# Turning the first batch's blocks by 16-bit halves and a transposing DMA instead of on TensorE

## The chip, the cores and the metric

One core of one Trainium2 chip runs the whole program. The metric is device microseconds of one execution; the time quoted for a kernel is the median of its runs.

## What is computed

The reference chains three layers for 2 batches of 768 positions with 512 channels. Banded attention gives x. A mixer follows, and then a second mixer with a rotation. The part that matters here is the first mixer:

```python
xt = x.transpose(0, 2, 1)
h = np.maximum(xt @ w_tok1, 0.0) @ w_tok2
u = x + h.transpose(0, 2, 1)
h2 = np.maximum(u @ w_ch1, 0.0) @ w_ch2
return (u + h2)
```

The product with `w_tok1` is called the first mixing product below, that with `w_tok2` the second. The product with `w_ch1` is the up-projection, that with `w_ch2` the down-projection.

## The kernel before

**Tiling.** A batch is held as x[b], six row blocks of 128 positions by 512 channels. Every large product is made of three passes: both operands are split into a high part (rounded to fp32r) and a low part (what is left), and `mm3` (L96) issues high*high, high*low and low*high.

**The stages around the change.** Attention runs in 24 units (each two blocks of one pair of heads), written out by hand in `attention_band`. The PE work of later layers is hung into its last units by the table `fill`: `token_part` is one step of the first mixing product (program names mm1, shown as mm), `token_row` one row block of the second (mm2, also shown as mm), whose result VectorE adds into x (L768, x<-mm). So batch 0 is through its second mixing product when attention ends, and batch 1 gets its own in `token_mix2`, behind the end of the If block that chooses between two forms of attention.

**The turn.** The up-projection needs u with channels on the partitions. Batch 0 is turned by `turn_row`: four 128x128 transposes on TensorE (L799, ut<-ident,x) into one PSUM bank of the tag "t" (two banks, which attention's own transposes t use too), then `evac_split`: ScalarE writes the high part (L706, xh<-ut), VectorE the low part (L712, xl<-ut,xh). The results lie in `ut[0]`, in two pieces: positions 0 to 511 (blocks 0 to 3) and 512 to 767 (blocks 4 and 5). Batch 1 is turned later, under batch 0's channel mix, in another way: GpSimd copies the block apart into 16-bit halves (L779, `halves_out`), the SP queue issues a transposing DMA (L783), GpSimd joins the halves again (L789, `halves_join`), then ScalarE writes the high part (L792) and VectorE the low part (L793).

**Conversions.** Weights come as 64-bit words and pass through jobs: a load on the SP queue (L125), two scaling steps on ScalarE (L139, L140), two steps on VectorE (L145, L148), an addition on GpSimd (L149), the high part on ScalarE (L157), the low part on VectorE (L160). Each call of `tick()` moves every running job one phase on and starts one more. Jobs of the channel mix are started by `token_mix2` (three ticks) and then by `up`, behind each of its two evacuations.

**The channel mix.** `up(b, k)` makes 128 hidden columns in two PSUM tiles gp of the tag "t" (two banks, so a third tile waits until the first is evacuated); each is evacuated by ScalarE (L706, g<-gp) and VectorE (L708). `down` accumulates into six banks (h).

All engines run their instructions in the order in which the program is written; nothing is rescheduled.

## Time and profile before

| | us |
|---|---|
| median of 3 runs (492.0 to 493.21) | 492.08 |
| the profiled execution, its own time | 493.28 |
| span of that execution, first to last instruction | 491.5 |
| PE (matmul) busy | 484.3 of 491.5 |
| DVE / ACT / POOL busy | 317.4 / 262.9 / 180.8 |

In a timeline a row shows start and duration in us from the start of the span, engine, line, operation, the tiles as out<-in, shapes and a count; what stands in square brackets is the engine's idle time ahead of it and what ended that. Median and profiled execution are different runs: differences worked out on the span are carried over to the median.

### The profile page before, as it was taken

To read this page: it belongs to the slowest core of one execution; us is meant where nothing else is said; L and a number is where in the kernel's file an instruction comes from. 1 tells how busy PE (TensorE), PEld (TensorE's weight loads), DVE (VectorE), ACT (ScalarE), POOL (GpSimd) and SP (SyncE) were. 2 spreads that over 40 slices of the span, in tenths; PEclk is the share of its full clock that TensorE was granted. 3 is DMA by queue.
4 is the path that set the end of the run, shared out by engine and by line. 5 is a ranking of instruction groups with operands and counts; after the bars stand their busy time and mean duration, and the time that the engine had idled before them with its cause. 6 is when DMAs were issued, how large, how long until landed. Compare 5 with 4: busy or idle time off the path is not lost.

```text
span 491.5 us, 7645 instructions
## 1 busy us (share of the span) xinstructions
PE 484.3 (99%) x2836; PEld 412.3 (84%) x2836; DVE 317.4 (65%) x671; ACT 262.9 (53%) x482; POOL 180.8 (37%) x187
## 2 busy tenths in 40 slices
PE   8999999999999999999999999999999999999997
PEld 4788888787888888888888888888888889988896
DVE  4688787854776689506656564687998866351442
ACT  6888777723565554204569464646776566322010
POOL 7345534430443575401323241334554633333000
PEclk9999999999999999999999999999999999999999
DMA  6687863401454545302444222524210101000012
GB/s 194 202 261 219 280 209 119 129 2 50 134 172 107 158 137 143 94 1 85 147 133 149 87 56 60 141 87 104 68 23 22 44 22 23 21 23 22 23 71 101
DMA packets 49022, 50.66 MB, mean 103 GB/s; under 512 B 20944, under 2 KB 39888, under 8 KB 48976
## 3 DMA queue, kind: packets, MB, share of 16 engines
q1 hardware_dynamic: 48976, 50.08, 34.6%
q8 instruction: 25, 0.41, 0.3%
q14 instruction: 21, 0.17, 0.1%
HBM read 42.21 MB, written 3.15 MB: 92 GB/s over the span
## 4 chain that ended last, share of the span: by engine, by line
PE 83%; DVE 5%; ACT 5%; POOL 3%; DMA 2%; issue 1%; DVEq 0%; SPq 0%; POOLq 0%; ACTq 0%
PE gp L96 20%; PE h L96 18%; PE y L96 13%; PE v L96 7%; PE mm L96 7%; PE o L406 5%; PE th L96 5%; PE t L484 4%; PE s L437 4%; DMA k<-k 2%; POOL base L319 1%; ACT cut_xt L789 1%; DVE x L1061 1%; DVE w L1154 1%; POOL s L1180 1%
## 5 line engine op out<-in xcount | busy, mean ns | idle before, releaser
L149 POOL TENSOR_TENSOR cvt<-cvt,cvs 128x512 int32<-128x512 int32 (+1 forms) x57 | 75.1, 1318 | 177.2 <-DVE cvt L148 144.0
L96 PE MATMUL h<-wc,g 128*128 128x512 f32 x432 | 101.7, 389 | 0.0
L96 PE MATMUL gp<-xh,wc 128*128 128x512 f32 (+1 forms) x384 | 97.1, 335 | 0.0
L96 PEld LDWEIGHTS h<-wc,g 128*128 128x128 f32 x432 | 79.6, 188 | 15.2
L96 PEld LDWEIGHTS gp<-xh,wc 128*128 128x128 f32 x384 | 67.2, 189 | 8.6 <-DVE g L708 0.2
L708 DVE SCALAR_TENSOR_TENSOR g<-gp,g 128x512 fp32r<-128x512 f32 (+1 forms) x48 | 26.7, 556 | 63.4 <-ACT g L706 63.1
L96 PE MATMUL gp<-xl,wc 128*128 128x512 f32 (+1 forms) x192 | 64.3, 335 | 0.0
L96 PE MATMUL y<-wri,s 128*128 128x256 f32 (+1 forms) x288 | 52.0, 335 | 0.2 <-POOL s L1180 0.2
L96 PE MATMUL y<-wri,z 128*128 128x256 f32 (+1 forms) x288 | 51.9, 335 | 0.0
L706 ACT ACTIVATE g<-gp 128x512 fp32r<-128x512 f32 (+1 forms) x48 | 23.4, 486 | 53.2 <-PE gp L96 53.2
L96 PEld LDWEIGHTS y<-wri,s 128*128 128x128 f32 x288 | 44.7, 189 | 6.4 <-POOL s L1180 0.4
L96 PEld LDWEIGHTS y<-wri,z 128*128 128x128 f32 x288 | 44.6, 188 | 5.9
L484 PE MATMUL t<-ident,e 128*128 128x128 f32 x176 | 48.1, 285 | 0.4 <-ACT at L496 0.4
L145 DVE SCALAR_TENSOR_TENSOR cvs<-cvt,cvs 128x512 int32<-128x512 int32 (+1 forms) x57 | 44.8, 787 | 0.1
L96 PEld LDWEIGHTS gp<-xl,wc 128*128 128x128 f32 x192 | 36.0, 188 | 4.7
L450 DVE CUSTOM_DVE_ANT_0 e<-s,base 128x256 f32<-128x256 f32 (+1 forms) x96 | 32.9, 397 | 9.1 <-PE s L437 7.1
L484 PEld LDWEIGHTS t<-ident,e 128*128 128x128 f32 x176 | 31.7, 184 | 8.1 <-issue 2.3
L139 ACT ACTIVATE cvt<-raw 128x512 f32<-128x512 f32 (+1 forms) x57 | 37.2, 653 | 2.2 <-issue 2.2
L140 ACT ACTIVATE cvs<-raw 128x512 int32<-128x512 uint16 (+1 forms) x57 | 37.4, 656 | 0.0
L96 PE MATMUL th<-s,xt 128*128 128x512 f32 x144 | 34.9, 391 | 0.0
L1157 ACT ACTIVATE w<-w 128x512 f32<-128x512 f32 x12 | 7.6, 632 | 49.4 <-DVE w L1154 49.4
L406 PE MATMUL o<-v,at 128*128 128x65 f32 x192 | 32.3, 252 | 0.0
(111 smaller groups left out, 839.9 us busy)
## 6 DMA issues: line engine op xcount, KB each, us to landing
raw<-w_ch SPq DMA_DIRECT2D x28, 512.0 KB, 4.1
raw<-w_tok SPq DMA_DIRECT2D x21, 512.0 KB, 4.2
k<-k SPq DMA_DIRECT2D x7, 480.0 KB, 5.6
v<-v SPq DMA_DIRECT2D x8, 384.0 KB, 3.7
out<-o SPq DMA_DIRECT2D x11, 256.0 KB, 2.0
q<-q SPq DMA_DIRECT2D x7, 384.0 KB, 4.7
raw<-w_theta SPq DMA_DIRECT2D x4, 512.0 KB, 4.0
a<-v SPq DMA_DIRECT2D x8, 240.0 KB, 4.5
```

What stands on the lines that cost most here:

```text
L96: self.nc.tensor.matmul(out, lhsT=a, rhs=b, start=first and i == 0, stop=last and i == n - 1)
L139: nc.scalar.activation(out=f(t), in_=f(top), func=AF.Copy, scale=2.0**-111)
L140: nc.scalar.activation(out=s, in_=nxt, func=AF.Copy, scale=2.0**-13)
L145: nc.vector.scalar_tensor_tensor(out=s, in0=t, scalar=-(1 << 31), in1=s, op0=ALU.bitwise_and, op1=ALU.bitwise_or)
L149: nc.gpsimd.tensor_tensor(out=t, in0=t, in1=s, op=ALU.add)
L406: self.nc.tensor.matmul(po[:, j * OW : j * OW + D + 1], lhsT=at, rhs=v[:, j * (D + 1) : (j + 1) * (D + 1)], start=first, stop=last,)
L437: nc.tensor.matmul(ps[j][:, ii, c0:], lhsT=t["q"][pj, i * P : (i + 1) * P], rhs=kf[pj, i * KW - P + c0 : i * KW + P], start=True, stop=True,)
L450: nc.vector.tensor_tensor_reduce(out=e, in0=ps[j][:, ii, c0:], in1=self.base[2 * hp + j][min(i, 1)], op0=ALU.add, op1=ALU.min, scale=-SCAL ...
L484: nc.tensor.transpose(pt[:, ii, c, :], e[j][:, ii, c * P : (c + 1) * P], self.ident)
L706: nc.scalar.activation(out=hi, in_=ps, func=AF.Relu if relu else AF.Copy)
L708: nc.vector.scalar_tensor_tensor(out=lo, in0=ps, scalar=0.0, in1=f(hi), op0=ALU.max, op1=ALU.subtract)
L1157: nc.scalar.activation(out=a, in_=t, func=AF.Abs)
```

## The change

Batch 0's blocks are no longer turned on TensorE. `turn_row` and `turn_rows` are gone, with their 24 transposes and 6 evacuations. In `token_mix2`, behind the If, all six blocks are cut into halves by GpSimd (`columns_out`), each followed by its transposing DMA on the SP queue; behind batch 1's second mixing product all six are joined (the first four by GpSimd, the last two by ScalarE) and split into high and low parts; the three ticks stand behind all that. The scratch lies in places that later hold converted weights. The first mixing product of batch 1 finishes its first half before its second half begins, and the second mixing product's first three rows are made in two passes, so that the first pass needs only that first half.

```diff
-            for s in range(4):
-                fill[N - 2 + s].append(columns(s))
-            for tb in range(NT):
-                for s in range(NS - 2):
-                    fill[N + 1].append(mix1(1, tb, s, "s"))
+            for s in range(NS - 2):
+                fill[N + 1].append(mix1(1, 0, s, "s"))
...
             for tb in range(NT):
-                for s in range(NS - 2, NS):
+                for s in range(0 if tb else NS - 2, NS):
                     mix1(1, tb, s, "s")()
-            for s in range(4, NS):
-                columns(s)()
...
-    def token_row(self, tag, h1, b, s):
-
-        ps = self.ps.tile([P, E], F32, name="mm2_%d_%d" % (b, s), tag=tag)
+    def token_row(self, tag, h1, b, s, parts=range(NT)):
+
         cs = slice(s * P, (s + 1) * P)
+        if 0 in parts:
+            self.mm2[b, s] = self.ps.tile([P, E], F32, name="mm2_%d_%d" % (b, s), tag=tag)
+        ps = self.mm2[b, s]
...
-                for t in range(NT)
+                for t in parts
             ],
-        )
-        x = self.x[b][:, s, :]
-        self.nc.vector.tensor_tensor(out=x, in0=ps, in1=x, op=ALU.add)
...
+            first=0 in parts,
+            last=NT - 1 in parts,
+        )
+        if NT - 1 in parts:
+            x = self.x[b][:, s, :]
+            self.nc.vector.tensor_tensor(out=x, in0=ps, in1=x, op=ALU.add)
...
     def token_mix2(self, h1):
+        pool, act = self.nc.gpsimd.tensor_copy, self.nc.scalar.copy
         for s in range(NS):
+            if s < 3:
+                t = self.ws.tile([P, 2, NE, P], F32, name="cut_u0_%d" % s, tag="w", bufs=9)
+            else:
+                t = self.split_raw(s - 1, "cut_u0_%d" % s)[:, 0 : 2 * E]
+                t = t.rearrange("p (l d x) -> p l d x", l=2, d=NE)
+            self.columns_out(0, s, t)
+        for t in range(NT):
+            for s in range(NS // 2):
+                self.token_row("acc", h1, 1, s, [t])
+        for s in range(NS // 2, NS):
             self.token_row("acc", h1, 1, s)
-            if s % 2:
-                self.tick()
...
+        for s in range(NS):
+            self.halves_join(self.turning[0, s], pool if s < 4 else act)
+            self.columns_split(0, s)
+        for _ in range(3):
+            self.tick()
```

How the instructions stand, at three places. First TensorE at the end of attention, where the row blocks 4 and 5 of batch 0 were turned (mm_1_0 and mm_1_1 are the two halves of batch 1's first mixing product); before:

```order
L96 MATMUL mm_1_1_1734<-xh_72,w_85 128x512 x2
L96 MATMUL mm_1_1_1734<-xl_73,w_85 128x512
L96 MATMUL mm_1_1_1734<-xh_72,w_85 128x512
L799 MATMUL ut_4_1763<-ident,x_65 128x128 x4
L799 MATMUL ut_5_1770<-ident,x_65 128x128 x4
L918 UNCONDITIONAL_BRANCH
```

and with the change:

```order
L96 MATMUL mm_1_1_1714<-xl_73,w_85 128x512
L96 MATMUL mm_1_1_1714<-xh_72,w_85 128x512 x2
L96 MATMUL mm_1_1_1714<-xl_73,w_85 128x512
L96 MATMUL mm_1_1_1714<-xh_72,w_85 128x512
L905 UNCONDITIONAL_BRANCH
```

The eight transposes ahead of the branch are gone; sixteen more are gone from the last four units in the same way.

Second VectorE behind the If, from the fourth addition of the second mixing product (x_66 is batch 1) to the first evacuation of the up-projection (g); before:

```order
L768 TENSOR_TENSOR x_66<-mm_1_3_7531,x_66 128x512
L145 SCALAR_TENSOR_TENSOR cvs_7518<-cvt_7517,cvs_7518 128x512
L148 TENSOR_SCALAR cvt_7517<-cvt_7517 128x512
L768 TENSOR_TENSOR x_66<-mm_1_4_7548,x_66 128x512
L768 TENSOR_TENSOR x_66<-mm_1_5_7556,x_66 128x512
L145 SCALAR_TENSOR_TENSOR cvs_7543<-cvt_7542,cvs_7543 128x512
L148 TENSOR_SCALAR cvt_7542<-cvt_7542 128x512
L708 SCALAR_TENSOR_TENSOR g_0_7585<-gp_0_0_7586,g_0_7585 128x512
```

and with the change, from the sixth addition:

```order
L764 TENSOR_TENSOR x_66<-mm_1_5_7475,x_66 128x512
L784 TENSOR_TENSOR xl_71<-cut_u_0_7417,xh_70 128x4x128
L784 TENSOR_TENSOR xl_71<-cut_u_1_7420,xh_70 128x4x128
L784 TENSOR_TENSOR xl_71<-cut_u_2_7423,xh_70 128x4x128
L784 TENSOR_TENSOR xl_71<-cut_u_3_7426,xh_70 128x4x128
L784 TENSOR_TENSOR xl_71<-cut_u_4_7429,xh_70 128x4x128
L784 TENSOR_TENSOR xl_71<-cut_u_5_7432,xh_70 128x4x128
L145 SCALAR_TENSOR_TENSOR cvs_7502<-cvt_7501,cvs_7502 128x512
L148 TENSOR_SCALAR cvt_7501<-cvt_7501 128x512
L145 SCALAR_TENSOR_TENSOR cvs_7511<-cvt_7510,cvs_7511 128x512
L148 TENSOR_SCALAR cvt_7510<-cvt_7510 128x512
L699 SCALAR_TENSOR_TENSOR g_0_7537<-gp_0_0_7538,g_0_7537 128x512
```

All six low parts of `ut[0]` (xl_71) now stand behind the sixth addition, and both conversion steps of the first two jobs behind those.

Third ScalarE behind the If, to the first evacuation of the up-projection; before:

```order
L139 ACTIVATE cvt_7517<-raw_7497 128x512
L140 ACTIVATE cvs_7518<-raw_7497 128x512
L139 ACTIVATE cvt_7542<-raw_7499 128x512
L140 ACTIVATE cvs_7543<-raw_7499 128x512
L157 ACTIVATE wc_0_7564<-cvt_7517 128x512
L139 ACTIVATE cvt_7569<-raw_7521 128x512
L140 ACTIVATE cvs_7570<-raw_7521 128x512
L706 ACTIVATE g_0_7585<-gp_0_0_7586 128x512
```

and with the change, from the fourth high part:

```order
L783 CAST xh_70<-cut_u_3_7426 128x4x128
L780 COPY cut_u_4_7429<-cut_u_4_7429 128x2x512
L783 CAST xh_70<-cut_u_4_7429 128x4x128
L780 COPY cut_u_5_7432<-cut_u_5_7432 128x2x512
L783 CAST xh_70<-cut_u_5_7432 128x4x128
L139 ACTIVATE cvt_7501<-raw_7413 128x512
L140 ACTIVATE cvs_7502<-raw_7413 128x512
L139 ACTIVATE cvt_7510<-raw_7415 128x512
L140 ACTIVATE cvs_7511<-raw_7415 128x512
L157 ACTIVATE wc_0_7516<-cvt_7501 128x512
L139 ACTIVATE cvt_7521<-raw_7505 128x512
L697 ACTIVATE g_0_7537<-gp_0_0_7538 128x512
```

Six high parts and two joins went ahead of the first scaling step; what stands between that step and the evacuation g is as before.

## Rows read from the trace of the kernel before

**Rows 1.** Stretches: busy us and instructions per engine, granted clock, DMA share, GB/s.

```profile
250.00:300.00 50.00, 50.00 (x248) 42.25 (x248) 29.39 (x49) 31.03 (x51) 16.45 (x12) 1.00 0.38 111
489.00:491.50 2.50, 0.00 (x0) 0.00 (x0) 0.00 (x0) 0.00 (x0) 0.00 (x0) 1.00 0.15 52
```

**Rows 2.** Timeline of TensorE, 92 to 107 us: start, us, instruction, count, idle before.

```profile
92.36 0.60 PE L799 MATMUL ut<-ident,x 128*128 128x128 f32 x4
92.89 1.13 PE L437 MATMUL s<-k,q 64*128 64x256 f32 x8
...
97.33 0.60 PE L799 MATMUL ut<-ident,x 128*128 128x128 f32 x4
98.31 0.33 PE L484 MATMUL t<-ident,e 128*128 128x128 f32 x1 [0.38 <-ACT at L496]
...
102.32 0.60 PE L799 MATMUL ut<-ident,x 128*128 128x128 f32 x4
102.75 0.33 PE L406 MATMUL o<-a,at 128*128 128x65 f32 x2
...
105.93 0.60 PE L799 MATMUL ut<-ident,x 128*128 128x128 f32 x4
106.28 0.48 PE L96 MATMUL mm<-xh,w 128*128 128x512 f32 x1
```

**Rows 3.** Timeline of TensorE, 114 to 125 us, and of its weight loads at 128.75.

```profile
114.58 1.03 PE L799 MATMUL ut<-ident,x 128*128 128x128 f32 x8
116.15 8.46 PE L96 MATMUL mm<-h,w 128*128 128x512 f32 x36 [0.54 <-ACT xh L706]
124.45 0.39 PE L96 MATMUL gp<-xh,wc 128*128 128x512 f32 x1
...
128.75 0.19 PEld L96 LDWEIGHTS gp<-xh,wc 128*128 128x128 f32 x1 [0.20 <-DVE g L708]
```

**Rows 4.** Timeline of VectorE, 115 to 128 us.

```profile
115.40 0.69 DVE L708 SCALAR_TENSOR_TENSOR h<-mm,h 128x512 fp32r<-128x512 f32 x1 [0.67 <-ACT h L706]
...
119.51 1.89 DVE L768 TENSOR_TENSOR x<-mm,x 128x512 f32<-128x512 f32 x3 [2.22 <-PE mm L96]
...
124.65 0.69 DVE L768 TENSOR_TENSOR x<-mm,x 128x512 f32<-128x512 f32 x1 [0.37 <-PE mm L96]
125.26 0.68 DVE L145 SCALAR_TENSOR_TENSOR cvs<-cvt,cvs 128x512 int32<-128x512 int32 x1
125.98 0.43 DVE L148 TENSOR_SCALAR cvt<-cvt 128x512 int32<-128x512 int32 x1
```

**Rows 5.** Timeline of ScalarE, 118 to 128 us.

```profile
118.52 0.66 ACT L139 ACTIVATE cvt<-raw 128x512 f32<-128x512 f32 x1 [2.17 <-issue]
...
125.16 0.63 ACT L157 ACTIVATE wc<-cvt 128x512 fp32r<-128x512 f32 x1 [4.31 <-POOL cvt L149]
...
126.25 0.65 ACT L140 ACTIVATE cvs<-raw 128x512 int32<-128x512 uint16 x1
127.37 0.60 ACT L706 ACTIVATE g<-gp 128x512 fp32r<-128x512 f32 x1 [0.47 <-PE gp L96]
```

**Rows 6.** Timeline of GpSimd: attention's last instruction, and one addition of a job.

```profile
106.19 0.74 POOL L382 TENSOR_TENSOR xl<-x,xh 128x256 fp32r<-128x256 f32 x1
...
126.55 1.29 POOL L149 TENSOR_TENSOR cvt<-cvt,cvs 128x512 int32<-128x512 int32 x1 [1.43 <-DVE cvt L148]
```

**Rows 7.** Batch 1's turn (cut_ut): ns min/median/max, first and last start, forms.

```profile
L779 POOL COPY cut_ut<-x x6: 1037/1258/1486, 155.6 to 199.8; 128x1024 uint16<-128x1024 uint16 x6
L789 POOL COPY cut_ut<-cut_ut x6: 1338/1590/1857, 163.8 to 204.1; 128x1024 uint16<-128x1024 uint16 x6
L793 DVE TENSOR_TENSOR xl<-cut_ut,xh x6: 677/936/1187, 171.6 to 208.1; 128x512 fp32r<-128x512 f32 x6
...
DMA to landing us min/median/max: 2.7/2.7/3.3
```

**Rows 8.** A join on ScalarE, in the last stage (cut_xt).

```profile
L789 ACT COPY cut_xt<-cut_xt x12: 1341/1354/1372, 258.4 to 417.2; 128x1024 uint16<-128x1024 uint16 x12
```

More of the change, by code (lines that the diff above doesn't have):

```diff
@@ L699, in attention_dense @@
                 self.token_row("m", h1, 0, s)
-                self.turn_row("t", 0, s)
     def evac_split(self, hi, lo, ps, relu=False):
@@ L763, in token_row @@
                 )
-                for t in range(NT)
+                for t in parts
             ],
-        )
-        x = self.x[b][:, s, :]
-        self.nc.vector.tensor_tensor(out=x, in0=ps, in1=x, op=ALU.add)
-    def turn_row(self, tag, b, s):
-        h, s0 = divmod(s * P, E)
-        hi, lo = (t[h][:, :, s0 : s0 + P] for t in self.ut[b])
-        self.turn_rows(tag, self.x[b][:, s, :], r(hi), r(lo), "ut_%d_%d" % (b, s))
+            first=0 in parts,
+            last=NT - 1 in parts,
+        )
+        if NT - 1 in parts:
+            x = self.x[b][:, s, :]
+            self.nc.vector.tensor_tensor(out=x, in0=ps, in1=x, op=ALU.add)
     def halves_out(self, src, t, copy):
@@ L793, in halves_split @@
         self.nc.vector.tensor_tensor(out=lo, in0=t[:, 1], in1=f(hi), op=ALU.subtract)
-    def turn_rows(self, tag, src, hi, lo, name):
-        pt = self.ps.tile([P, NE, P], F32, name=name, tag=tag)
-        for d in range(NE):
-            self.nc.tensor.transpose(pt[:, d, :], src[:, d * P : (d + 1) * P], self.ident)
-        self.evac_split(hi, lo, pt)
     def token_jobs(self):
@@ L826, in split_tile, with split_raw @@
         m = n // 3
+        c0 = (0 if m % 2 else SHIFT) if narrow else (GRAIN - SHIFT if m % 2 else 0)
+        w = self.split_raw(m, name)
+        return w[:, c0 : c0 + 2 * E].rearrange("p (l e) -> p l e", l=2)
+    def split_raw(self, m, name):
         size = 2 * E + (GRAIN if m == 4 else (SHIFT, GRAIN - SHIFT)[m % 2])
-        c0 = (0 if m % 2 else SHIFT) if narrow else (GRAIN - SHIFT if m % 2 else 0)
-        w = self.ws.tile([P, size], F32, name=name, tag="n%d" % m)
-        return w[:, c0 : c0 + 2 * E].rearrange("p (l e) -> p l e", l=2)
+        return self.ws.tile([P, size], F32, name=name, tag="n%d" % m)
     def channel_piece(self, pool, k, half):
@@ L882, in run @@
                 self.ut.append((self.columns_of(2 * b, hi), self.columns_of(2 * b + 1, lo)))
-            self.mm1 = {}
+            self.mm1, self.mm2 = {}, {}
             self.ps = Banks(es.enter_context(tc.tile_pool(name="ps", bufs=1, space=PSUM)))
@@ L996, in moe @@
         self.moe_jobs(ws, w12p)
+        self.turning = {}
         self.prefetch()
@@ L1005, in token_mix2, with columns_out, columns_split @@
     def token_mix2(self, h1):
+        pool, act = self.nc.gpsimd.tensor_copy, self.nc.scalar.copy
         for s in range(NS):
-            self.token_row("acc", h1, 1, s)
-            if s % 2:
-                self.tick()
-    def columns_out(self, pb, s):
-        t = self.turning[s] = pb.scratch("ut_%d" % s, ("cut", "xt0", "xt1")[s % 3])
-        self.halves_out(self.x[1][:, s, :], t, self.nc.gpsimd.tensor_copy)
-    def columns_split(self, s):
+            if s < 3:
[8 more added lines that the diff above has]
+        for s in range(NS // 2, NS):
+            self.token_row("acc", h1, 1, s)
+        for s in range(NS):
[3 more added lines that the diff above has]
+            self.tick()
+    def columns_out(self, b, s, t):
+        self.turning[b, s] = t
+        self.halves_out(self.x[b][:, s, :], t, self.nc.gpsimd.tensor_copy)
+    def columns_split(self, b, s):
         h, s0 = divmod(s * P, E)
-        hi, lo = (u[h][:, :, s0 : s0 + P] for u in self.ut[1])
-        self.halves_split(self.turning.pop(s), r(hi), r(lo))
+        hi, lo = (u[h][:, :, s0 : s0 + P] for u in self.ut[b])
+        self.halves_split(self.turning.pop((b, s)), r(hi), r(lo))
     def channel_mix(self, gp, pb):
@@ L1072, in channel_mix @@
                 if 0 <= k - 4 < NS:
-                    self.columns_split(k - 4)
+                    self.columns_split(1, k - 4)
                 if 0 <= k - 3 < NS:
-                    self.halves_join(self.turning[k - 3], nc.gpsimd.tensor_copy)
+                    self.halves_join(self.turning[1, k - 3], nc.gpsimd.tensor_copy)
                 if 0 <= k - 2 < NS:
-                    self.columns_out(pb, k - 2)
+                    s = k - 2
+                    self.columns_out(1, s, pb.scratch("ut_%d" % s, ("cut", "xt0", "xt1")[s % 3]))
             if b == 1:
```

3 lines of the change are left out of this document (removed).

## The prediction

> **What bounds the kernel now.** I read the stretches first [rows 1]: from 250 to 300 us PE is busy 50.00 of 50.00 us at a granted clock of 1.00. PE is the bound, so a microsecond taken from its queue is a microsecond of the kernel, as long as nothing makes PE wait instead, and a microsecond lost early on is not won back. So I ask two things of the stretch from 92 to 133 us: what goes out of PE's queue, and which wait stands at its head afterwards. The timeline of PE [rows 2, 3] shows the 24 transposes. The timelines of VectorE and ScalarE [rows 4, 5] show how narrow the hand-over to the up-projection is already: the sixth addition of the second mixing product starts 0.20 us after PE has gone on to gp (124.65 against 124.45), and ScalarE had only 0.47 us to spare before its first evacuation g. All sums are made on the profiled span, 491.5 us (that execution took 493.28 us as a whole; the median is 492.08). What I find as a difference is added to the median.
>
> **The change part by part: what goes.** Sixteen transposes stood in attention's last units. The four groups held PE from 92.36 to 92.89, 97.33 to 98.31, 102.32 to 102.75 and 105.93 to 106.28 [rows 2]: 0.53 + 0.98 + 0.43 + 0.35 = 2.29 us. The second holds a wait of 0.38 us for ScalarE's copy at. I count it as gone: attention's transposes t share two banks with ut, and without ut the next one takes a bank that was freed one copy earlier. The bare pitch of a transpose, (1.03 - 0.60)/4 = 0.11 us from a group of eight and one of four [rows 2, 3], makes 16 x 0.11 = 1.7 us the lower bound. I take 2.2.
>
> The other eight stood between batch 1's two mixing products, 114.58 to 116.15 [rows 3]. Not all of that 1.57 us is won. The second half's low part h ends at 115.40 + 0.69 = 116.09 [rows 4], and the second mixing product must wait for it. The change lets three matmuls run ahead of it, from the first half alone. In the built program the fourth waits for that second h, although its own data are ready. So 33 of 36 matmuls start where all 36 started: 3 x 8.46/36 = 0.7 us won (0 if the branch at the If costs PE that much, 0.9 at best). Together PE is **2.9 us** earlier at the up-projection, at 121.55 instead of 124.45, with bounds of 1.8 and 3.2.
>
> **What comes: first wait.** PE's second matmul of gp takes the low part xl. VectorE makes all six xl behind the sixth addition, because it works in program order. That addition starts 0.20 us after PE is done, at 121.75. VectorE's pitch is (1.89 - 0.69)/2 = 0.60 us [rows 4], so xl of block 0 starts at 122.35, of block 3 at 124.15, and this ends at 124.84. PE wants it at 121.55 + 0.23 = 121.78. It waits **3.1 us**, and is then 0.2 us behind the kernel before: the first wait alone eats the gain. In the kernel before nothing waited there, as xl was made under attention's matmuls.
>
> **Second wait.** The third up tile needs the bank of the first, so it needs g evacuated. In front of g on ScalarE stands the first job's high part, L157, which needs GpSimd's addition, which needs VectorE's L145 and L148, which now stand behind all six xl. The chain: xl of block 5 ends at 124.15 + 1.20 + 0.69 = 126.04; L145 and L148 take 1.15 from start to end (125.26 to 125.98 + 0.43, [rows 4]), to 127.2; the addition 1.29 [rows 6], to 128.5; from the start of L157 over two scaling steps to g's earliest start 126.25 + 0.57 - 125.16 = 1.66 [rows 5], to 130.15; from g's start over VectorE's low part to PE's next weight load 128.75 - 127.37 = 1.38 [rows 3, 5]. The third tile starts at 131.55, before it was 128.75: **2.8 us** behind.
>
> One thing can stretch that. A VectorE instruction with two operands in SBUF, xl of batch 1, took 677 ns in some cases and 1187 in others [rows 7], the long ones where a GpSimd instruction ran. Here the second job's L145, of the same kind, starts just when GpSimd's addition would. That is 0.5 us more, so 3.3 us behind. The Trainium skill (SBUF — State Buffer, section Who interferes with whom) says that such a VectorE instruction and a GpSimd instruction that reads SBUF exclude each other, and that the one that starts first holds the port for all of its time; the trace's two durations agree. By that rule the sum is 3.3, without it 2.8.
>
> From there PE is full again, and both kernels do the same in the same order. No row shows an idle PE that could give the time back. So the sum is +2.8 to +3.3, of which I take the upper, with a span of 494.8 and a median of 492.08 + 3.3 = **495.4 us**. With the bounds of the gain it runs from 492.08 + 2.5 to 492.08 + 4.4.
>
> **What I cost at nothing, and its cover.** GpSimd is done with attention at 106.93 [rows 6], or about 105 now. Even with a start after the If as late as ScalarE's (2.17 us of "issue", [rows 5]) its six copies of 1.04 [rows 7] find the time. The sixth is held until the second h is stored, at about 113.9 (116.09 - 2.2): the wait counts that were set for the other form of attention reach that far. So the joins start at 114.9, the fourth ends at 114.9 + 4 x 1.34 = 120.3, its high part at 120.9; VectorE wants that at 124.15: 3.2 us of cover. The six transposing DMAs land 2.7 us after issue [rows 7], behind each other on the SP queue, the last by about 118, when ScalarE's first join is not yet due. Behind them on that queue stands the third weight load, which starts no later than before. ScalarE then has two joins of 1.35 [rows 8] and two high parts of 0.60, to 124.8; xl of block 5 wants that at 125.35, and its first scaling, done at about 126, is wanted by L145 at 126.05. There the cover is thin: whatever makes the joins later by more than a few tenths moves the second wait one for one. The 24 transposes' evacuations on ScalarE and VectorE go too, but those had room.
>
> **Rivals.** *The second wait is covered, the time is about the same.* If g were evacuated in time, +0.2 is left, 492.3 us. It decides at whether the chain behind xl of block 5 (126.04 to 131.55, 5.5 us) is shorter than PE's work ahead of the third tile (4.3 us from gp's start, 128.75 - 124.45, less the 1.2 us by which block 5 comes after block 3: 3.1 us). It isn't, by 2.4 us; 7%.
>
> *The gain stays, the kernel is faster.* Were PE not held at gp, 492.08 - 2.9 = 489.2 us. That needs the six xl to be made before the sixth addition; the joins could feed them from 116 us on, but VectorE's queue stands in another order. 5%.
>
> *The joins come late and meet VectorE.* If GpSimd's sixth copy takes 1.48 instead of 1.04 and its joins 1.86 instead of 1.34 [rows 7], the fourth join ends 0.44 + 4 x 0.52 = 2.5 us later. The first wait still stays (cover 3.2), but ScalarE's first scaling is 2.4 us later than VectorE's L145 wants it, and the second wait grows by that: 497.8 us. It decides from about 0.1 us of delay on. Against it: the long ones of those rows lie beside VectorE's work on two SBUF operands, and VectorE has none of that before xl. 10%.
>
> *The waits cost the clock as well.* PE now stands for about 3 us twice within 10 us, which the kernel before never does. In the last stretch [rows 1] there is no matmul for 2.50 us and the granted clock still reads 1.00, its upper level, which speaks against. If it fell to the lower of its two levels, half, in one of the waits, the matmuls behind it would take twice as long for a while: 2 to 4 us more, about 498. The Trainium skill (TensorE: Matmul & The Clock Gate, section Why this matters for your kernels) warns of idle gaps of about this size between bursts of matmuls, after which the clock goes to half; no run here shows it yet. 10%.
>
> **How the numbers follow.** The two waits as I size them get 68%: 494.5 to 496.5. Late joins and the clock are slower still, 10% each. The covered second wait is the same within 0.3% (1.5 us, about what a measurement of this kernel can tell from no change), 7%, and 2% of the forecast's own range may end there too; the kept gain is faster, 5%. So faster 0.05, same 0.09, slower 0.86. For eight in ten the range goes from 493.8, where gain and waits lie at their kind bounds, to 498.0, which takes in the late joins and half of the clock's case.
>
> **What would show each step.** In the profile of the changed kernel: batch 1's first mixing product starts near 104.1 instead of 106.28; gp's first matmul near 121.6; an idle PE of about 3 us behind it, ended by VectorE's xl (L784); a second one of 2.5 to 3.5 us ahead of the third up tile, ended by VectorE's g (L699); from there on the same distance to the kernel before, to the end. I would be wrong if the first wait is ended by ScalarE or GpSimd (then the joins bound), if there is no second wait, or if the granted clock reads below 1.00 behind one of them.

## The result and the profile after

The changed kernel takes 496.59 us (median of 4 runs, 496.37 to 497.33) against 492.53 us for the kernel before in the same comparison: a ratio of 1.0081, 95% interval 1.0069 to 1.0093. The profiled execution took 496.62 us, its span is 494.8 us, and PE was busy 483.7 us of it, 0.6 us less than before: the change takes work from PE, and PE waits for more than it saves.

The timeline of the changed kernel, all engines, from batch 1's first product to the first down-projection (start, duration, engine, instruction, count, idle before and what ended it):

```profile
104.28 0.40 PE L96 MATMUL mm<-xh,w 128*128 128x512 f32 x1
...
114.03 7.79 PE L96 MATMUL mm<-h,w 128*128 128x512 f32 x33 [0.71 <-DVE h L699]
114.04 1.04 POOL L770 COPY cut_u<-x 128x1024 uint16<-128x1024 uint16 x1 [3.04 <-DVE h L699]
115.03 5.13 POOL L780 COPY cut_u<-cut_u 128x1024 uint16<-128x1024 uint16 x4
...
118.78 3.77 DVE L764 TENSOR_TENSOR x<-mm,x 128x512 f32<-128x512 f32 x6 [4.80 <-issue]
118.80 2.19 ACT L783 CAST xh<-cut_u 128x512 fp32r<-128x512 f32 x4 [5.55 <-issue]
...
121.66 0.39 PE L96 MATMUL gp<-xh,wc 128*128 128x512 f32 x1
...
122.47 3.69 DVE L784 TENSOR_TENSOR xl<-cut_u,xh 128x512 fp32r<-128x512 f32 x6
...
125.01 0.80 PE L96 MATMUL gp<-xl,wc 128*128 128x512 f32 x1 [2.96 <-DVE xl L784]
...
126.08 0.68 DVE L145 SCALAR_TENSOR_TENSOR cvs<-cvt,cvs 128x512 int32<-128x512 int32 x1
...
127.31 1.66 POOL L149 TENSOR_TENSOR cvt<-cvt,cvs 128x512 int32<-128x512 int32 x1 [7.16 <-DVE cvt L148]
...
129.00 0.63 ACT L157 ACTIVATE wc<-cvt 128x512 fp32r<-128x512 f32 x1 [1.92 <-POOL cvt L149]
...
130.65 0.58 ACT L697 ACTIVATE g<-gp 128x512 fp32r<-128x512 f32 x1
...
131.27 0.69 DVE L699 SCALAR_TENSOR_TENSOR g<-gp,g 128x512 fp32r<-128x512 f32 x1 [2.01 <-ACT g L697]
...
132.01 0.50 PE L96 MATMUL gp<-xh,wc 128*128 128x512 f32 x1 [1.34 <-DVE g L699]
...
136.28 0.61 PE L96 MATMUL h<-wc,g 128*128 128x512 f32 x2
```

Read it against [rows 3 to 5]. PE comes to gp at 121.66 instead of 124.45. VectorE's six low parts xl, one group of 3.69 us, now stand behind its six additions, and gp's second matmul waits 2.96 us for them. L145 stands behind the low parts, GpSimd's L149 behind L145, ScalarE's L157 behind that, and g behind two more scaling steps (L139 and L140, at 129.54 and 130.10 in the trace; the order shown for ScalarE has only the first of them): 126.08, 127.31, 129.00, 130.65, 131.27 are one chain, and the third up tile starts at 132.01 where it started at 128.75.

The stretches of the same execution (PE, PEld, DVE, ACT and POOL busy us, then the granted clock, DMA share, GB/s) show what the wait of 1.34 us ahead of the third tile hides:

```profile
121.60:124.85 3.25, 0.45 (x2) 0.03 (x1) 3.25 (x6) 3.19 (x5) 0.00 (x0) 1.00 0.01 3
124.85:128.25 3.40, 3.24 (x8) 2.56 (x9) 3.33 (x7) 2.24 (x4) 0.94 (x1) 0.50 0.25 83
128.25:132.00 3.75, 2.43 (x17) 2.06 (x15) 1.74 (x3) 3.00 (x6) 2.02 (x2) 1.00 0.69 218
```

Behind the first wait the granted clock is 0.50, which is 1.2 GHz, for 3.4 us, and most of the first up tile runs at half pace. The kernel before had 1.00 in all of this stretch:

```profile
100.00:140.00 40.00, 39.46 (x208) 33.34 (x207) 23.79 (x42) 17.41 (x32) 9.79 (x11) 1.00 0.27 81
```

For the experiments I cut every kernel's span at four of PE's starts: the scores of attention's second unit from the end (87.63 in the kernel before, 87.40 in the changed one), batch 1's first product mm, the up-projection gp, and the first down-projection h. All are read from PE's timeline of each profiled execution; fill matmuls count as gp.

| kernel | scores to mm | mm to gp | gp to h | h to the end | median, us | ratio to before, 95% interval |
|---|---|---|---|---|---|---|
| before | 18.65 | 18.17 | 8.57 | 358.5 | 492.5 | |
| changed | 16.88 | 17.38 | 14.62 | 358.5 | 496.59 | 1.0069 to 1.0093 |
| order_alone | 18.64 | 18.05 | 8.57 | 358.6 | 492.38 | 0.9989 to 1.0007 |
| two_blocks | 18.65 | 17.48 | 8.67 | 358.4 | 492.25 | 0.9985 to 1.0003 |
| adds_last | 16.87 | 17.36 | 17.47 | 358.6 | 499.07 | 1.0119 to 1.0150 |
| conversions_first | 16.87 | 18.50 | 13.08 | 358.6 | 495.94 | 1.0059 to 1.0086 |
| conversions_first_fill | 16.87 | 17.36 | 12.87 | 358.5 | 494.61 | 1.0028 to 1.0057 |
| fill_first_wait | 16.87 | 17.42 | 15.91 | 358.6 | 497.88 | 1.0087 to 1.0116 |
| both_moved | 16.87 | 17.39 | 13.24 | 360.4 | 496.67 | 1.0071 to 1.0098 |
| sixth_copy_freed | 16.87 | 17.37 | 14.78 | 358.6 | 496.88 | 1.0071 to 1.0097 |
| freed_and_moved | 16.87 | 17.39 | 14.54 | 358.8 | 496.56 | 1.0068 to 1.0094 |
| no_transposing_dma | 16.88 | 17.37 | 14.61 | 358.5 | 496.17 | 1.0059 to 1.0091 |
| interleaved | 16.87 | 17.37 | 9.39 | 359.1 | 492.87 | 0.9994 to 1.0017 |
| interleaved_2 | 16.87 | 17.59 | 10.14 | 358.5 | 492.54 | 0.9982 to 1.0002 |

The first column holds the sixteen transposes in attention: 18.65 with them, 16.87 without, in every kernel. The second holds the other eight. The third is where the change loses. The fourth is 358.5 in the kernel before and in the changed one: nothing of the loss is given back.

### The profile page after: what moved, and what is told of

It is laid out like the page before. It is cut to its first block, busy times and chain, and to the rows that moved or that the text cites. A ratio compares the mean times of both kernels' runs of the same rounds, so it can differ in the third digit from the quotient of the medians.

```text
span 494.8 us, 7631 instructions
## 1 busy us (share of the span) xinstructions
PE 483.7 (98%) x2812; PEld 410.4 (83%) x2812; DVE 317.1 (64%) x671; ACT 265.5 (54%) x484; POOL 192.1 (39%) x197
## 4 chain that ended last, share of the span: by engine, by line
PE 84%; DVE 8%; ACT 5%; POOL 1%; issue 1%; DVEq 0%; ACTq 0%
PE gp L96 19%; PE h L96 18%; PE y L96 13%; PE v L96 7%; PE mm L96 6%; PE o L406 6%; PE s L437 5%; PE th L96 5%; PE t L484 4%; PE warm L330 1%; ACT cut_xt L780 1%; DVE xl L784 1%; DVE x L1063 1%; DVE cvs L145 1%; ACT cvt L139 1%
## 5 line engine op out<-in xcount | busy, mean ns | idle before, releaser
L149 POOL TENSOR_TENSOR cvt<-cvt,cvs 128x512 int32<-128x512 int32 (+1 forms) x57 | 75.5, 1325 | 166.1 <-DVE cvt L148 135.8
L145 DVE SCALAR_TENSOR_TENSOR cvs<-cvt,cvs 128x512 int32<-128x512 int32 (+1 forms) x57 | 44.9, 788 | 0.1
L140 ACT ACTIVATE cvs<-raw 128x512 int32<-128x512 uint16 (+1 forms) x57 | 37.4, 656 | 0.0
L139 ACT ACTIVATE cvt<-raw 128x512 f32<-128x512 f32 (+1 forms) x57 | 37.3, 654 | 0.0
```

The costliest lines, as they stand in the source:

```text
L139: nc.scalar.activation(out=f(t), in_=f(top), func=AF.Copy, scale=2.0**-111)
L140: nc.scalar.activation(out=s, in_=nxt, func=AF.Copy, scale=2.0**-13)
L145: nc.vector.scalar_tensor_tensor(out=s, in0=t, scalar=-(1 << 31), in1=s, op0=ALU.bitwise_and, op1=ALU.bitwise_or)
L149: nc.gpsimd.tensor_tensor(out=t, in0=t, in1=s, op=ALU.add)
```

## The experiments

The theory: VectorE works its queue off in program order, and the change made that queue longer between the second mixing product and the first evacuation g. Rivals: the transposed blocks come too late by themselves (joins, DMAs, the start behind the branch); the clock; and each wait counting for itself.

**adds_last.** Take the first wait away and leave the second. `token_add` is the addition split off from `token_row`.

```diff
...
-            self.token_row("acc", h1, 1, s)
+            self.token_row("acc", h1, 1, s, add=False)
...
             self.halves_join(self.turning[0, s], pool if s < 4 else act)
+            if s == 4:
+                for n in range(4):
+                    self.token_add(1, n)
             self.columns_split(0, s)
+        for n in range(4, NS):
+            self.token_add(1, n)
```

> The changed kernel with one thing moved: VectorE's additions of batch 1's second mixing product stand behind the low parts xl (the first four behind xl of block 3, the last two behind xl of block 5); the conversions stay behind both. Theory (the second wait alone sets the end, the first is swallowed by it): gp's second matmul waits under 0.6 us instead of 2.96, L145 still starts near 126.1 to 126.7, PE then waits some 5 to 6 us ahead of the third up tile, which starts near 132.0 to 132.6; time 496.6, within 0.7 of the changed kernel. Rival 1 (each wait costs what it lasts): 3 us faster, 493.6. Rival 2 (the clock's price shows once the wait is in one piece): as the theory, but the matmuls behind the third tile run at 1.2 GHz for some 3.4 us, 1.7 us more, 498.3.

Measured 499.07 us, slower still. Its timeline of PE, and its stretches from the third tile on:

```profile
122.16 0.50 PE L96 MATMUL gp<-xl,wc 128*128 128x512 f32 x1 [0.49 <-DVE xl L787]
...
125.75 0.39 PE L96 MATMUL gp<-xl,wc 128*128 128x256 f32 x1 [0.69 <-DVE xl L787]
...
132.71 0.79 PE L96 MATMUL gp<-xh,wc 128*128 128x512 f32 x1 [5.42 <-DVE g L699]
...
138.75 0.63 PE L96 MATMUL h<-wc,g 128*128 128x512 f32 x2
```

```profile
127.25:132.70 5.45, 0.04 (x1) 0.00 (x0) 3.38 (x6) 2.99 (x6) 2.91 (x2) 0.73 0.56 174
132.70:136.30 3.60, 3.59 (x9) 2.82 (x10) 3.56 (x6) 1.75 (x5) 1.28 (x1) 0.50 0.62 211
```

The first wait shrank from 2.96 to 0.49 us and bought nothing: the third tile starts at 132.71 (0.70 later, as L145 came 0.74 later). So the waits don't add, and the chain behind the low parts sets the end. The clock now falls behind the second wait, and there it is paid for: from the third tile to h it is 6.04 us here and 4.27 in the changed kernel, 1.8 us more. The rival of the clock held its ground here, the rival of separate waits fell.

**fill_first_wait.** The same question from the other side: 13 extra matmuls keep PE at work in the first wait.

```diff
+                for _ in range(13 if (b, k, h) == (0, 0, 0) else 0):
+                    nc.tensor.matmul(
+                        ps, lhsT=r(c1[0][:, 0]), rhs=r(uth[0][:, 0]), start=True, stop=True
+                    )
                 self.mm3(
```

> The changed kernel with 13 extra matmuls (the first high times high product of the first up tile, overwritten by the real ones) at the place of the first wait. Theory (the clock's fall to 1.2 GHz behind the first wait costs nothing in the changed kernel, because the second wait takes the loss up): the granted clock stays at 1.00, the first up tile is done earlier, PE waits some 3 us ahead of the third tile instead of 1.34, that tile starts near 132.0 as before; time 496.6 within 0.5 us. Rival (the clock's loss of some 1.7 us is part of the slowdown): 494.9.

Measured 497.88 us, 1.3 us more than I expected. A row of its timeline of PE, and its stretch behind it:

```profile
132.15 0.80 PE L96 MATMUL gp<-xh,wc 128*128 128x512 f32 x1 [2.79 <-DVE g L699]
```

```profile
132.15:134.80 2.65, 2.65 (x6) 2.15 (x7) 2.62 (x5) 1.14 (x3) 0.97 (x1) 0.50 0.62 206
```

The third tile stays where it was (132.15) although the first tile ran at 2.4 GHz: so in the changed kernel the clock's fall behind the first wait costs nothing. What I had not expected is that it falls behind the second wait instead, once that one lasts 2.79 us. Three of the five executions had a mean clock of 0.997 and spans of 496.1 to 496.3, two had 1.000 and spans of 494.8 and 495.3: 1.1 us for the fall.

**conversions_first.** Take the second wait away and leave the first.

```diff
...
+        for s in range(NS):
+            self.token_add(1, s)
+            if s in (1, 3):
+                self.tick()
         for s in range(NS):
-            self.halves_join(self.turning[0, s], pool if s < 4 else act)
+            if s > 3:
+                self.halves_join(self.turning[0, s], act)
             self.columns_split(0, s)
-        for _ in range(3):
-            self.tick()
+        self.tick()
```

(GpSimd's four joins stand ahead of the second product's rows.)

> The changed kernel with the first two ticks put back between the additions as in the kernel before, GpSimd's joins ahead of them, the third tick behind the low parts. Theory: L145 and L148 of the first job run ahead of the six low parts, so the first wait grows by about 1.15 to some 4.1 us (gp's second matmul near 126.0) and the second wait is no longer ended by the chain from L145 over GpSimd to L157; g is free at 129.0 at the latest. The third up tile starts at 130.2 if the clock stays at 2.4 GHz and at 131.8 if it falls to 1.2 in the first wait as it did in the changed kernel; 494.8 or 496.4 us. Rival (the order of conversions and low parts is not what makes the second wait): a wait ahead of the third tile of over 1 us stays and the time is 496.6.

**conversions_first_fill** is that kernel with the 13 fill matmuls.

> conversions_first with the same 13 extra matmuls where its second matmul of gp waits. Theory (there no second wait follows, so the clock's fall is paid for): the granted clock stays at 1.00, the third up tile starts near 129.7 to 130.0 instead of 131.3, span 492.8 or a little less, time 494.4 against 495.9 without the fill. Rival (the fall of the clock costs nothing there either, or a chain through ScalarE's queue holds g): 495.9.

Measured 495.94 and 494.61 us. Two rows of conversions_first's timeline of PE:

```profile
122.52 0.50 PE L96 MATMUL gp<-xh,wc 128*128 128x512 f32 x1 [0.96 <-ACT xh L786]
125.57 0.80 PE L96 MATMUL gp<-xl,wc 128*128 128x512 f32 x1 [2.54 <-DVE xl L787]
```

Behind the second of these rows the granted clock is 0.51:

```profile
125.55:129.00 3.45, 3.43 (x8) 2.76 (x9) 2.28 (x4) 2.35 (x5) 0.88 (x1) 0.51 0.06 8
```

No wait stands ahead of the third tile any more: the second wait was indeed the place of the conversions in VectorE's queue. With the conversions ahead, the first wait is 0.96 + 2.54 = 3.5 us, and the time is within the uncertainty of the changed kernel's: taking away the second wait alone wins no more than can be told, either. With the fill the clock stays at 1.00 and 1.3 us are won. So the price of the fall is 1.1 to 1.8 us in three kernels where PE has no later wait to hide it in, and nothing in the changed one.

**both_moved.** Low parts of blocks 0 to 3 first, the conversion next, low parts 4 and 5, and additions in between; all joins on GpSimd; two ticks ahead instead of three.

```diff
...
+            self.halves_join(self.turning[0, s], pool)
+        self.token_add(1, 0)
+        for s in range(4):
+            self.columns_split(0, s)
+        self.token_add(1, 1)
+        self.token_add(1, 2)
+        self.tick()
+        self.tick()
+        for s in range(4, NS):
             self.columns_split(0, s)
...
```

> The changed kernel with both moved: behind the branch VectorE does one addition, the low parts of blocks 0 to 3, two additions, the first conversion's L145 and L148, the low parts of blocks 4 and 5, and the last three additions behind the first evacuation g; GpSimd makes all six joins; two ticks ahead of the channel mix and the third behind its second up tile. Theory (the turn off TensorE is worth its 2.8 us, the order of VectorE's queue ate it): gp's second matmul waits under 0.5 us, the third up tile starts near 126.2, the granted clock stays 1.00, span 488.9, time about 490.0 against 492.5 of the kernel before. Rival (the turn by DMA is too late whatever the order, since ScalarE and VectorE issue nothing until 118.8): a first wait of over 1.5 us stays and the time is 491.5 or more.

Measured 496.67 us: the theory's number was missed by 6.7 us. Its timeline, GpSimd, VectorE and PE:

```profile
115.08 8.07 POOL L783 COPY cut_u<-cut_u 128x1024 uint16<-128x1024 uint16 x6
...
120.18 4.67 DVE L787 TENSOR_TENSOR xl<-cut_u,xh 128x512 fp32r<-128x512 f32 x4
...
124.91 0.50 PE L96 MATMUL gp<-xl,wc 128*128 128x512 f32 x1 [2.80 <-DVE xl L787]
...
127.03 2.35 DVE L787 TENSOR_TENSOR xl<-cut_u,xh 128x512 fp32r<-128x512 f32 x2
...
127.19 1.64 POOL L149 TENSOR_TENSOR cvt<-cvt,cvs 128x512 int32<-128x512 int32 x1 [4.04 <-DVE cvt L148]
...
129.44 0.39 PE L96 MATMUL gp<-xl,wc 128*128 128x256 f32 x1 [1.62 <-DVE xl L787]
...
140.61 0.50 PE L96 MATMUL gp<-xh,wc 128*128 128x512 f32 x1 [1.41 <-DVE g L699]
```

Its stretch behind the first of these waits:

```profile
124.90:128.00 3.10, 2.91 (x12) 2.17 (x12) 3.07 (x6) 0.26 (x1) 0.81 (x1) 1.00 0.59 186
```

GpSimd's joins ran to 123.15. The first two low parts, which ran beside the last two joins, took 1.78 and 1.77 us, and the next two 0.68 each; the 1.17 of later forecasts is only the mean of the four. Of the last two low parts the first took 0.68 and the one beside L149 1.75. In the changed kernel six took 3.69 in all, because GpSimd was done. That is the exclusion that the prediction had from [rows 7], now in a place of its own, and the Trainium skill's rule for it (SBUF — State Buffer, section Who interferes with whom) agrees. The last row is the tick that I had moved: g of the second up step stood behind two jobs' steps.

**order_alone.** One part of the change alone: the transposes stay on PE, only the order of batch 1's products is the new one (the first three rows of the second in two passes, as in the change).

```diff
-            for tb in range(NT):
-                for s in range(NS - 2):
-                    fill[N + 1].append(mix1(1, tb, s, "s"))
+            for s in range(NS - 2):
+                fill[N + 1].append(mix1(1, 0, s, "s"))
...
```

> The kernel before, with its transposes on TensorE, and one part of the change alone: the first half of batch 1's first mixing product finished before the second half begins, and the first three rows of the second mixing product in two passes. Theory: worth little while the eight transposes stand between the two products, since they cover all but 0.54 us of that wait: 492.0 to 492.5, within 0.3% of the kernel before. Rival (the 0.7 us that the change wins there are the reordering's own): 491.8 and no wait at all between the products.

Measured 492.38 us, no difference; mm to gp took 18.05 against 18.17 us. So the order by itself wins nothing that can be told. The 0.8 us that the change wins there come with the eight transposes; no run takes these away and keeps the old order, so how much of the 0.8 needs both is open.

**two_blocks.** Half of the change: blocks 0 to 3 turned on PE, blocks 4 and 5 by the DMA, their low parts at the head of VectorE's queue.

```diff
-            for s in range(4, NS):
-                columns(s)()
...
+        for s in range(4, NS):
+            t = self.ws.tile([P, 2, NE, P], F32, name="cut_u0_%d" % s, tag="w", bufs=9)
+            self.columns_out(0, s, t)
+        for s in range(4, NS):
+            self.halves_join(self.turning[0, s], self.nc.gpsimd.tensor_copy)
+            self.columns_split(0, s)
```

> Half way between the two kernels: blocks 0 to 3 are turned on TensorE in attention as before, only blocks 4 and 5 by GpSimd and the transposing DMA; batch 1's products in the order of the change; the ticks between the additions as before; the two low parts at the head of VectorE's queue behind the branch. Theory (there is room for two low parts ahead of the additions, and only the eight transposes between the two products are gone): PE is at gp near 123.75 instead of 124.45, no wait at gp, third up tile near 128.1, granted clock 1.00; time 491.8 against 492.5, within what can just be told from no change. Rival (also two blocks come too late): a wait at gp or ahead of the third tile of 1 us or more, 493 or more.

Measured 492.25 us, ratio 0.9994 (0.9985 to 1.0003). No wait at gp or ahead of the third tile, mm to gp 0.69 us shorter than before, gp to h 0.10 longer. The profile shows the 0.6 us; the times can't tell them from nothing.

**sixth_copy_freed.** Do the joins bind? In the other form of attention batch 0's second product was put ahead of batch 1's first, so that GpSimd's sixth copy waits for less.

```diff
                         self.token_part("m", h1, bb, tb, s)
-            for s in range(NS):
-                self.token_row("m", h1, 0, s)
+                if bb == 0:
+                    for s in range(NS):
+                        self.token_row("m", h1, 0, s)
```

> The changed kernel with one difference: in the other form of attention batch 0's second mixing product stands ahead of batch 1's first, so that GpSimd's sixth copy needn't wait for the second h. Copies done near 111.4, the last transposing DMA some 3 us earlier, GpSimd's joins from about 111.5 instead of 115.0. Theory (VectorE's queue order makes both waits, not the joins): time 496.6 within 0.5 us, first wait still near 3 us and ended by xl. Rival (the joins are what is late): 2 us or more faster, 494.6 or below. Beside it: if the silence of ScalarE and VectorE behind the branch (5.55 and 4.80 us) comes from the transposing DMAs, both issue again earlier, by 116.5; if it comes from the branch alone, at 118.8 as before.

Measured 496.88 us, first wait 2.96 us as before. But this run doesn't settle the question, since the joins hardly moved: the first starts at 113.70, 1.3 us earlier and not 3.5, and the fourth ends at 117.61 + 2.73 = 120.34, where it ended at 120.16 in the changed kernel. The new wait counts held the first copy to 107.81, and then the transposing DMAs came one by one (its timeline of GpSimd):

```profile
113.70 1.35 POOL L781 COPY cut_u<-cut_u 128x1024 uint16<-128x1024 uint16 x1
115.95 1.35 POOL L781 COPY cut_u<-cut_u 128x1024 uint16<-128x1024 uint16 x1 [0.90 <-DMA cut_u<-cut_u]
117.61 2.73 POOL L781 COPY cut_u<-cut_u 128x1024 uint16<-128x1024 uint16 x2 [0.31 <-DMA cut_u<-cut_u]
```

That the joins don't make the waits is to be read elsewhere: in the changed kernel VectorE's six low parts run in one piece, 0.60 us apart, so none of them waits for a join; and in no_transposing_dma below the first high part stands at 116.38 instead of 118.80, and the first wait is 2.97 us. The forecast beside it, on the silence behind the branch, is not decided here either: ScalarE and VectorE went on at 116.60 and 118.06.

**freed_and_moved** puts both_moved's order on top of that, with three ticks.

> sixth_copy_freed with VectorE's queue in this order behind the branch: one addition, the low parts of blocks 0 to 3, the first conversion's L145 and L148, the low parts of blocks 4 and 5, two additions, the second conversion's, the first evacuation g, the last three additions; all six joins on GpSimd; three ticks ahead of the channel mix. Theory (with the joins done before the low parts run, these take 0.60 us each instead of 1.17 and are ready when PE is): waits of PE from 121 to 142 us under 1.5 us in all, granted clock 1.00, third up tile near 126.5, span 488.8 to 490, time 490 to 491 against 492.5 of the kernel before. Rival (VectorE has too much to do there whatever the order, or issues too late behind the branch): waits of over 2.5 us in all and 492 or more.

Measured 496.56 us, by the rival's number. Because the DMAs came late, GpSimd's joins again ran beside VectorE's low parts (four took 5.82 us), gp's second matmul waited 2.67 us, and the clock fell behind it:

```profile
124.51 0.80 PE L96 MATMUL gp<-xl,wc 128*128 128x512 f32 x1 [2.67 <-DVE xl L788]
```

```profile
124.50:127.90 3.40, 3.39 (x8) 2.72 (x9) 3.37 (x5) 0.73 (x3) 1.66 (x1) 0.52 0.70 248
```

**no_transposing_dma.** Why are ScalarE and VectorE silent for 5.55 and 4.80 us behind the branch?

```diff
...
-        a = t[:, 1].rearrange("p d x -> p (d x)").bitcast(U16)
+        a = t[:, 1 if turn else 0].rearrange("p d x -> p (d x)").bitcast(U16)
...
-        self.nc.sync.dma_start_transpose(out=b.rearrange("p (m x) -> p m x", x=P), in_=a)
+        if turn:
+            self.nc.sync.dma_start_transpose(out=b.rearrange("p (m x) -> p m x", x=P), in_=a)
```

> The changed kernel without batch 0's six transposing DMAs: the copies write straight to where the joins read, so batch 0's blocks are not turned and all behind them is computed from wrong columns; every other instruction stays. Theory (the six DMAs hold up the code of ScalarE and VectorE behind the branch): ScalarE's first instruction comes about 3 us behind its branch, near 115.7 to 116.5 instead of 118.8, VectorE's near 116.5 instead of 118.8. Rival (the silence belongs to the branch alone): 118.8 as in the changed kernel. By both the time stays at 496.6 within 0.6, since VectorE's queue order makes the waits.

Measured 496.17 us. Its first rows on ScalarE and VectorE behind the branch, and its stretch of 105 to 119 us:

```profile
116.38 0.62 ACT L784 CAST xh<-cut_u 128x512 fp32r<-128x512 f32 x1 [3.15 <-POOL cut_u L781]
```

```profile
116.45 2.04 DVE L764 TENSOR_TENSOR x<-mm,x 128x512 f32<-128x512 f32 x3 [2.50 <-PE mm L96]
```

```profile
105.00:119.00 14.00, 13.27 (x59) 10.67 (x58) 3.52 (x6) 2.53 (x5) 10.16 (x11) 1.00 0.03 7
```

In the changed kernel the same stretch has a DMA share of 1.03 instead of 0.03:

```profile
105.00:119.00 14.00, 13.29 (x59) 10.60 (x58) 1.77 (x4) 1.39 (x3) 10.16 (x11) 1.00 1.03 109
```

From the branch instruction to the next one on ScalarE and VectorE the trace gives 2.8 and 3.1 us here, 2.8 to 3.1 in before, order_alone and two_blocks, and 3.5 to 6.1 in all ten kernels with six transposing DMAs. So what the silence has over some 3 us is the DMAs' doing. The Trainium skill (Runtime: NRT & Kernel Launch, section Instruction fetch mechanics) says that a taken branch to a far target makes the engine fetch its code by a DMA before it goes on; the runs agree, and show that this fetch gets slower in a crowd. On one of the trace's instruction queues an 8 KB packet follows each of the two branches: here they start at 113.54 and 114.30 us and take 0.57 and 0.38 us, in the changed kernel they start at 113.92 and 116.06 and take 2.18 and 0.97. (The trace doesn't name the engine that a packet is for; I go by the order.) In the changed kernel the silence costs nothing, as the time shows: additions that start 2.3 us earlier still end with the sixth, which PE's last row releases:

```profile
121.82 0.69 DVE L764 TENSOR_TENSOR x<-mm,x 128x512 f32<-128x512 f32 x1 [0.61 <-PE mm L96]
```

**interleaved.** Use both findings: no join beside a low part, and nothing queued that must wait.

```diff
+            if s == NS - 1:
+                for n in range(2):
+                    self.halves_join(self.turning[0, n], pool)
             self.columns_out(0, s, t)
...
+        for n in (2, 3):
+            self.halves_join(self.turning[0, n], pool)
+        self.columns_split(0, 0)
+        self.columns_split(0, 1)
+        self.halves_join(self.turning[0, 4], act)
+        self.columns_split(0, 2)
+        self.columns_split(0, 3)
+        self.token_add(1, 0)
+        self.token_add(1, 1)
...
```

> The changed kernel with its queues interleaved so that no join runs on GpSimd while VectorE makes low parts: GpSimd joins blocks 0 and 1 ahead of its sixth copy and 2 and 3 behind it; ScalarE behind the branch: high parts 0 and 1, join 4, high parts 2, 3 and 4, first scaling, join 5, high part 5, second scaling, g; VectorE: low parts 0 to 3, two additions, L145 and L148 of the first job, low parts 4 and 5, one addition, g, and the last three additions spread behind; two ticks ahead of the channel mix instead of three. Theory (only the order of the queues ate the 2.8 us won on TensorE): low parts 0 to 3 take 0.60 us each and are done by 121.9, gp's second matmul waits under 0.5 us, the waits of PE from 121 to 142 us stay under 1 us in all, third up tile near 126.4, span 489.2, time about 490.2. Rival (ScalarE and VectorE start too late behind the branch for so much work, whatever its order): waits of 2.5 us or more in all and 492.5 or more.

Measured 492.87 us: 3.7 us better than the changed kernel, and no better than before. Its rows on ScalarE, VectorE and PE:

```profile
116.96 1.14 ACT L786 CAST xh<-cut_u 128x512 fp32r<-128x512 f32 x2 [3.25 <-POOL cut_u L783]
```

```profile
118.84 2.50 DVE L787 TENSOR_TENSOR xl<-cut_u,xh 128x512 fp32r<-128x512 f32 x4 [4.41 <-DMA cut_u<-cut_u]
```

```profile
125.96 0.39 PE L96 MATMUL gp<-xl,wc 128*128 128x256 f32 x1 [0.86 <-DVE xl L1032]
```

Low parts 0 to 3 take 0.60 us each, the first wait is gone, the clock stays at 1.00, gp to h is down from 14.62 to 9.39 us. What is left are the 0.86 us for low part 5, which ran beside L149, and 0.6 us later on (359.1 to the end instead of 358.5): PE loses them in the up step from 193 to 198 us, behind the third tick, which I had put behind the seventh down-projection step.

**interleaved_2** is to mend these two; the third addition goes behind the first g as well.

```diff
+        self.halves_join(self.turning[0, 5], act)
...
         self.nc.vector.tensor_tensor(out=r(nlo), in0=t5[:, 1], in1=f(r(nhi)), op=ALU.subtract)
+        self.tick()
+        self.tick()
...
-            if (b, k) == (0, 6):
+            if (b, k) == (0, 1):
```

> interleaved with join 5 and high part 5 ahead of both scalings on ScalarE, so that VectorE makes low parts 4 and 5 ahead of L145 and not beside GpSimd's addition (there low part 5 took 1.79 us instead of 0.60, and PE waited 0.86 us for it), and with the third tick given back behind the second down-projection step instead of the seventh (there PE fell 0.56 us back near 196 us). Theory (what is left of the slowdown in interleaved are these two places): no wait over 0.3 us at gp, third up tile near 126.0 to 126.4 instead of 127.3, from the first down-projection to the end 358.5 us as in the kernel before, span 489.0, time about 491.0 against 492.5 of the kernel before. Rival (the turn's work on VectorE and ScalarE has to come out of the same stretch whatever the order): what is won at gp is waited for later, and the time stays at 492.6 or more.

Measured 492.54 us, ratio 0.9992 (0.9982 to 1.0002). The later loss is gone (358.5 to the end), but in the profiled execution ScalarE started behind the branch at 118.77 instead of 116.96, with all its work, and the third tile waited 0.88 us for g:

```profile
118.77 1.14 ACT L786 CAST xh<-cut_u 128x512 fp32r<-128x512 f32 x2 [5.17 <-DMA cut_u<-cut_u]
```

```profile
128.10 0.50 PE L96 MATMUL gp<-xh,wc 128*128 128x512 f32 x1 [0.88 <-DVE g L699]
```

Its spans go from 488.6 to 491.4 us over twelve executions. Its start behind the branch came 1.8 us apart from interleaved's; that this is the scatter's cause is likely, but I have one profile of each. No kernel here beats the one before by more than can be told.

## Why the prediction was right, and which term was off

**The time.** 495.4 us forecast, 496.59 measured: inside the range, 0.1 us above the band that I gave the two waits alone. Both waits are there, ended by the instructions that I named, and the third tile starts where the sum put it. But one of my own signs of being wrong came up, for the granted clock did fall behind the first wait, and the idle time ahead of the third tile came out at 1.34 us. I had not worked out that the second wait would take up what the clock costs; that this left the sum standing is luck.

**The gain from sixteen transposes: 2.2 forecast, 1.77 measured.** Between the same two instructions of attention and mm the transposes cost 18.65 - 16.88 = 1.77 us in every pair of kernels: 16 times the bare pitch of 0.11, which I had as the lower bound. The step that failed is the wait of 0.38 us that I "count as gone". It went, but PE now waits 0.47 us one instruction further on, for VectorE's x:

```profile
97.41 0.41 PE L406 MATMUL o<-a,at 128*128 128x65 f32 x2 [0.47 <-DVE x L399]
```

I also read the forecast off two groups' starts, where each group's hold on PE overlaps with what follows.

**The other eight: 0.7 forecast, 0.79 measured** (18.17 - 17.38). **gp's start: 121.55 forecast, 121.66 measured.** That is closer than the terms deserve: the kernel before reached the scores of the second last unit at 87.63, the changed one at 87.40, so 0.23 us of the 2.79 are scatter from earlier on.

**First wait: 3.1 forecast, 2.96 measured,** ended by xl as forecast. adds_last shows that it alone is worth nothing. My sentence "the first wait alone eats the gain" is true of the sum, but the two waits don't add.

**Second wait: third tile 3.3 us behind forecast, 3.26 measured** (132.01 against 128.75), with GpSimd's addition held up beside the second L145 as I took it, by 0.37 us where I had 0.5 (L149 1.66 instead of 1.29 us). conversions_first shows the cause by removing it. The idle time ahead of the tile was only 1.34 us, where I had said 2.5 to 3.5: the clock stretched the first tile into it.

**What I costed at nothing** held: the sixth copy at 114.04 (113.9 forecast), the joins done at 120.16 (120.3), and the low parts behind them never waited. For the start behind the branch I had only the 2.17 us of ScalarE in [rows 5] in mind; ScalarE and VectorE were silent for 5.55 and 4.80 us, and the two joins on ScalarE came just in time all the same.

**The rivals.** The clock did fall, which I gave 10% and 2 to 4 us. The mechanism was there, its price was nil, since a later wait for another engine took it up; 1.1 to 1.8 us is what it costs where none follows. The late joins did not happen. The covered second wait and the kept gain would have needed another order of VectorE's queue, as the prediction said; interleaved has nearly that order, and got 492.87 us, not 489.2.

**The sum.** Scores to h is 45.39 us before and 48.88 after: 3.5 us lost, 3.3 forecast. The medians differ by 4.06. The remaining 0.6 us are not in these stretches of the profiled executions. The start of that unit scatters by some 0.5 us either way (86.99 in order_alone, 87.63 in the kernel before), and I took the 3.3 us from an execution of 493.28 us and put them on a median of 492.08, while later runs of the same kernel have a median of 492.53. Against its own execution the sum gives 496.6. Whether the change also moves the part ahead of the scores stays open.

## What to carry to other kernels

When work is moved from the bound engine to others, write down the order of every queue that it enters, at the place where it enters: here 2.6 us were saved on TensorE and 6 us lost in waits and at the lower clock, because six instructions stood ahead of a conversion that a PSUM bank hung on. Two waits of the bound engine on one helper's queue don't add: here taking away either alone won nothing that could be told (499.07 and 495.94 against 496.59 us), and only an order of the queues that took away both brought 492.87. Look at what runs behind a branch with crowded DMA queues ahead of it: it starts later, though no kernel here was shown to lose time by it.

## What the runs showed of the hardware

- The code behind the branch came 2.8 to 3.1 us after it on ScalarE and VectorE with the DMA queues almost idle (a share of 0.03 in no_transposing_dma), and 3.5 to 6.1 us with six transposing DMAs under way.
- Transposing DMAs of 128x1024 16-bit elements, one after the other, took a median of 4.5 us from issue to landing, against 2.7 for the single ones of [rows 7].
- VectorE's low part, two operands in SBUF, took 0.68 us by itself and 1.75 to 1.79 beside an instruction of GpSimd (both_moved, interleaved).
- The granted clock stood at 1.2 GHz behind waits of PE of 2.96 us (changed kernel), 2.79 (fill_first_wait), 5.42 (adds_last), 2.67 (freed_and_moved) and 2.54 with one of 0.96 just ahead of it (conversions_first). It stayed at 2.4 GHz behind one of 2.80 in both_moved's profiled execution. So the length of the wait alone doesn't tell which it will be. In [rows 1] it read 1.00 in 2.50 us without a matmul, but none followed there.
